# A recurrent-attention and MoE kernel on one core: weight casts on ScalarE, first loads in the modelled queue, products of zeros in TensorE's idle head, DMA transposes for blocks 14 to 23

## The chip, the cores and the metric

The kernel runs on one core of one Trainium2 chip. The metric is the device time of one execution in microseconds (us). The profile is one execution taken by the hardware profiler; its span is about 1.8 us shorter than the timed run. Most runs of one kernel here lie within 1 to 2% of each other.

## The reference

Two stages follow each other. For each of 4 batches and 8 heads, with 768 steps and head size 48:

```python
for t in range(S):
    state = alpha[:, :, t, :, None] * state + einsum('bhd,bhe->bhde', k[:, :, t], v[:, :, t])
    y[:, :, t] = einsum('bhd,bhde->bhe', q[:, :, t], state)
x = y.transpose(0, 2, 1, 3).reshape(B * S, H * D)        # 3072 tokens x 384
h = x @ w_in                                             # 384 x 2048
g = s * max(h, 0) ** 2 + b
out = g @ w_out                                          # 2048 x 384
```

## The kernel before

The 3072 tokens are 24 blocks of 128. For each block the kernel takes the logarithm of alpha (Ln), sums it over time with a matmul, exponentiates it, scales q and k, transposes both, and makes a masked score matrix and a running state. This "attention" of a block takes about 2 us of TensorE at full rate. Then come two dense layers in bf16: `mm1` (1.5k columns per unit, 96 units, 0.65 us each) and `mm2` (96 quarters of a block, 0.65 us each). Weights arrive as fp32 in eight quarters of 768 KB, four of w_in (i0 to i3) and four of w_out (o0 to o3); each is cast to bf16 before use.

Every step is an entry `op(engine, duration, priority, function, reads, writes)`. A small list scheduler in the kernel replays these entries with modelled durations, and the instructions are then emitted in the order of their modelled begin times. On the chip each engine runs its own instructions strictly in that order. If the model believes that a load lands earlier than it does, the engine stops at the instruction that needs it, with ready work behind.

```python
LEAD = {1: 17.0, 2: 20.0, 4: 18.0}         # how far a block's attention runs ahead, in units of 1.65 us
NST = 4                                    # staging buffers for fp32 weights
LOADS = ["b0", "b1", "i0", "i1", "b2", "i2", "b3", "i3", "o0", "o1", "o2", "b4", "o3", "b5", "b6"]

class Schedule:
    def emit(self):
        begin = self.run()                                  # list scheduling, durations in us
        for i in sorted(range(len(self.ops)), key=lambda i: (begin[i], i)):
            self.ops[i][3](*self.ops[i][4])                 # emit in this order
# [...]
    load(0, alpha, a_in); load(0, q, q_in); load(0, k, k_in); load(0, v, v_in)   # block 0, before the scheduler
# [...]
    def cast_w_in(i, st):
        nc.gpsimd.tensor_copy(out=w_in_bf[...], in_=wst[st].rearrange("a (k f) -> a k f", k=3))
# [...]
    def st_T(n):                                            # q and k of a block, on TensorE
        for x, src in ((0, qb_sb[n % 2]), (1, kb_sb[n % 2])):
            f = src.rearrange("a h d -> a (h d)")
            for p in range(NP):
                nc.tensor.transpose(out=t_ps[:, x, p, :], in_=f[:, 128 * p : 128 * p + 128], identity=ident_bf)
# [...]
            if i == 0:                                      # block 0: "landed at 3.5, 4.5, 5.5, 6.5"
                for x, name in enumerate("aqkv"):
                    sched.done((name, 0), 3.5 + x)
# [...]
            op("SP", 2.1, t, load_w_in, i, st, w=[("wst", st)], lat=2.0)
            op("POOL", 1.45, -500, cast_w_in, i, st, r=[("wst", st)], w=[("wib", i)])
# [...]
                    op("SP", 0.98, rank + 0.1 * x, load, n, src, dst, w=[(name, ii)], lat=2.0)
```

Because block 0's four loads are not entries, the modelled load queue is free at time 0, so the model has every later load some 5 us too early (the change enters them with 2.2 + 3 x 0.98 = 5.1 us).

Of the kernel before, what the change touches and what calls it, by code (L numbers as in the profile page):

```python
# [9 lines left out]
BF16 = mybir.dt.bfloat16  # L10
AF = mybir.ActivationFunctionType
# [6 lines left out]
GROUPS = [2, 2, 2, 2, 4, 4, 4, 4]  # L18
LEAD = {1: 17.0, 2: 20.0, 4: 18.0}

# [3 lines left out]

LOADS = ["b0", "b1", "i0", "i1", "b2", "i2", "b3", "i3", "o0", "o1", "o2", "b4", "o3", "b5", "b6"]

class Schedule:
# [79 lines left out]

    def emit(self):
        begin = self.run()
        for i in sorted(range(len(self.ops)), key=lambda i: (begin[i], i)):  # L110
            self.ops[i][3](*self.ops[i][4])


@with_exitstack
def kernel(
# [63 lines left out]

    load(0, alpha, a_in)  # L180
    load(0, q, q_in)
    load(0, k, k_in)
    load(0, v, v_in)
    nc.scalar.preload_act_table_set("natural_log_exp_and_others")
# [4 lines left out]
    ident_bf = sb.tile([128, 128], BF16, name="ident_bf")  # L189
    make_identity(nc, ident_bf)  # L190
    ones_col_bf = sb.tile([128, 1], BF16, name="ones_col_bf")
    nc.vector.memset(ones_col_bf, 1.0)
    vp_sb = many("vp", 3, [128, NP, VW], BF16, zero=nc.gpsimd)
    mask = sb.tile([128, 128], BF16, name="mask")
    make_upper_triangular(nc, mask, 1.0, diag=True)
    b_sb = many("b_s", 2, [128, H, D], FP32)
    binv_sb = many("binv", 2, [128, H, D], FP32)
    qb_sb = many("qb", 2, [128, H, 64], BF16, zero=nc.vector)
    kb_sb = many("kb", 2, [128, H, 64], BF16, zero=nc.vector)
    qkT_sb = many("qkT", 2, [128, 2, NP, 128], BF16)  # L200
    am_sb = many("am", 2, [128, 2, NP, 128], BF16)
# [25 lines left out]
    def cast_w_in(i, st):  # L227
        nc.gpsimd.tensor_copy(
            out=w_in_bf[:, :, QW // 3 * i : QW // 3 * (i + 1)],
            in_=wst[st].rearrange("a (k f) -> a k f", k=3),  # L230
        )

# [6 lines left out]
    def cast_w_out(i, st):  # L239
        nc.gpsimd.tensor_copy(  # L240
            out=w_out_bf[:, 4 * i : 4 * i + 4],
            in_=wst[st].rearrange("a (j m) -> a j m", j=4),
        )

# [56 lines left out]
    def st_vcast(n):  # L301
        nc.gpsimd.tensor_copy(
            out=vp_sb[n % 3].rearrange("a p (x d) -> a p x d", d=D)[:, :, 0:3:2, :],
            in_=v_in[n % NIN].rearrange("a (p e) d -> a p e d", e=2),
        )

    def st_qb(n):
        nc.vector.tensor_tensor(  # L308
            out=qb_sb[n % 2][:, :, 0:D], in0=q_in[n % NIN], in1=b_sb[n % 2], op=ALU.mult
        )  # L310

    def st_kb(n):
        nc.vector.tensor_tensor(
            out=kb_sb[n % 2][:, :, 0:D],
            in0=k_in[n % NIN],
            in1=binv_sb[n % 2],
            op=ALU.mult,
        )

    def st_T(n):  # L320
        for x, src in ((0, qb_sb[n % 2]), (1, kb_sb[n % 2])):
            f = src.rearrange("a h d -> a (h d)")
            for p in range(NP):
                nc.tensor.transpose(  # L324
                    out=t_ps[:, x, p, :],
                    in_=f[:, 128 * p : 128 * p + 128],
                    identity=ident_bf,
                )

    def st_KV(n):  # L330
        kb = kb_sb[n % 2].rearrange("a h d -> a (h d)")
        vp = vp_sb[n % 3]
        for p in range(NP):
            for e in range(2):
                nc.tensor.matmul(  # L335
                    out=p_ps[64 * e : 64 * e + 64, p, :],
                    lhsT=kb[:, 128 * p + 64 * e : 128 * p + 64 * e + 64],
                    rhs=vp[:, p, 48 * e : 48 * e + 96],
                    start=True,
                    stop=True,  # L340
                )

    def st_Tcopy(n):
        nc.vector.tensor_copy(  # L344
            out=qkT_sb[n % 2].rearrange("a x p t -> a (x p t)"),
            in_=t_ps.rearrange("a x p t -> a (x p t)"),
        )
# [18 lines left out]
    def st_A(n):  # L366
        qkT = qkT_sb[n % 2]
        for p in range(NP):
            for e in range(2):
                nc.tensor.matmul(  # L370
                    out=a_ps[:, e, p, :],
                    lhsT=qkT[64 * e : 64 * e + 64, 1, p, :],
                    rhs=qkT[64 * e : 64 * e + 64, 0, p, :],
                    start=True,
                    stop=True,
                )
# [22 lines left out]
    def st_y(n):  # L399
        first = n % NCH == 0  # L400
        qT = qkT_sb[n % 2][:, 0]
        am = am_sb[n % 2]
        vp = vp_sb[n % 3]
        st = s_sb[(n - 1) % 2]
# [104 lines left out]
    def first(n):  # L509
        return n % NCH == 0  # L510
# [10 lines left out]
    for rank, item in enumerate(loads):  # L521
        t, i = rank - 1000, int(item[1:])
        if item[0] == "b":
            if i == 0:
                for x, name in enumerate("aqkv"):
                    sched.done((name, 0), 3.5 + x)
                op("POOL", 0.5, t + 0.5,
# [9 lines left out]
        if item[0] == "i":  # L537
            op("SP", 2.1, t, load_w_in, i, st, w=[("wst", st)], lat=2.0)
            op("POOL", 1.45, -500, cast_w_in, i, st, r=[("wst", st)], w=[("wib", i)])
        else:  # L540
            op("SP", 2.1, t, load_w_out, i, st, w=[("wst", st)], lat=2.0)
            op("POOL", 1.45, -400, cast_w_out, i, st, r=[("wst", st)], w=[("wob", i)])
            op("DVE", 0.85, -5, colsum_part, i, st, r=[("wst", st)],
               w=["colpart" if i else "colsum"])
            if i:
                op("DVE", 0.85, -5, colsum_add, r=["colpart"], w=["colsum"])
# [4 lines left out]
    for g in range(NG):  # L551
        m = GROUPS[g]
        ring = [(first_blk[g] + x) % RING for x in range(m)]
        for n in range(first_blk[g], first_blk[g] + m):
# [11 lines left out]
            op("ACT", 0.55, t + 0.1, st_exp_i, n, r=["ct"], w=[("bi", i2), ("bl", i2)])  # L566
            op("POOL", 0.6, t + 0.2, st_vcast, n, r=[("v", ii)], w=[("vp", i3)])
            op("DVE", 0.47, t + 0.2, st_qb, n, r=[("q", ii), ("b", i2)], w=[("qb", i2)])
            op("DVE", 0.47, t + 0.2, st_kb, n, r=[("k", ii), ("bi", i2)], w=[("kb", i2)])
            op("PE", 0.5, t + 0.3, st_T, n, r=[("qb", i2), ("kb", i2)], w=["ct"], lat=0.27)  # L570
            op("DVE", 0.61, t + 0.4, st_Tcopy, n, r=["ct"], w=[("qkT", i2)])
            op("PE", 0.34, t + 0.35, st_KV, n, r=[("kb", i2), ("vp", i3)], w=["py"], lat=0.27)
            if first(n):
                op("DVE", 0.48, t + 0.5, st_t1, n, r=["py", ("bl", i2)], w=[("S", i2)])
            elif not last(n):
                op("DVE", 0.48, t + 0.5, st_t1, n, r=["py", ("S", 1 - i2)], w=[("t1", i2)])
                op("POOL", 0.9, t + 0.1, st_snew, n, r=[("t1", i2), ("bl", i2)], w=[("S", i2)])
            op("PE", 0.33, t + 0.5, st_A, n, r=[("qkT", i2)], w=["a"], lat=0.27)
            op("DVE", 1.15, t + 0.6, st_mask, n, r=["a"], w=[("am", i2)])
            rr = [("am", i2), ("qkT", i2), ("vp", i3)] + ([] if first(n) else [("S", 1 - i2)])  # L580
            op("PE", 0.55, t + 0.7, st_y, n, r=rr, w=["py"], lat=0.27)
# [13 lines left out]
        for u in range(4 * m):  # L595
# [8 lines left out]
            if jq == 3:  # L604
                op("DVE", 0.54, t + 0.1, oevac, x, r=[("o", ob), "bias", "s"],
                   w=[("os", (x // 4) % 3)])
                op("SP", 0.7, -2000, ostore, x, r=[("os", (x // 4) % 3)])
    sched.emit()

# [29 lines left out]
```

## Time and profile before

| | before |
|---|---|
| time, median | 217.84 us (217.25 to 218.16, 3 runs) |
| span of the profile | 215.9 us |
| last matmul starts | 212.10 us |

The table of stages of the kernel before follows. Its columns are: the stretch in us from the span's start, its length, then busy us (and instructions) of TensorE, TensorE's weight loads, VectorE, ScalarE and GpSimd, then the granted TensorE clock, the busy share of the DMA engines, and GB/s.

```profile
core 0: us, PE busy (x) PEld busy (x) DVE busy (x) ACT busy (x) POOL busy (x), PEclk, DMA share, GB/s
0.00:10.00 10.00, 0.56 (x5) 0.41 (x5) 1.64 (x7) 2.50 (x4) 5.18 (x17) 1.00 0.81 157
10.00:20.00 10.00, 6.48 (x74) 4.39 (x75) 7.44 (x10) 2.79 (x9) 4.07 (x4) 1.00 0.95 264
20.00:30.00 10.00, 7.49 (x67) 4.82 (x65) 5.93 (x10) 3.68 (x10) 4.72 (x5) 1.00 0.92 252
30.00:40.00 10.00, 6.85 (x72) 4.32 (x70) 8.09 (x11) 2.17 (x4) 7.51 (x5) 0.83 0.99 276
40.00:50.00 10.00, 7.02 (x66) 4.19 (x64) 10.00 (x18) 4.43 (x10) 2.79 (x3) 0.84 0.98 226
50.00:60.00 10.00, 10.00 (x113) 6.72 (x110) 9.30 (x23) 6.46 (x15) 3.02 (x4) 0.98 0.64 134
60.00:80.00 20.00, 20.00 (x244) 13.97 (x243) 15.76 (x36) 11.52 (x26) 3.93 (x6) 1.00 1.02 207
```

Two regimes meet near 52 us. From there TensorE is full, and only less TensorE work can shorten the rest. Before that TensorE is busy 7 of 10 us at best while the DMA engines are above 90%, and VectorE is full from 40 to 50 us. This is the "head". A busy TensorE is also not a fast one here, as the next lines show.

Timeline of the kernel before, TensorE, the same six mm1 matmuls twice (columns: start us, us, engine, line, operation, output<-inputs, shape, count):

```profile
24.85 1.46 PE L454 MATMUL h_ps_66<-xd_146,w_in_bf 128*128 128x256 bf16 x6
31.16 0.83 PE L454 MATMUL h_ps_66<-xd_146,w_in_bf 128*128 128x256 bf16 x6
```

The first group ran "cold", at about half the rate. The column for the granted clock says 1.00 for 20 to 30 us, so it does not show this; durations do. TensorE was cold once more at the very end of the head (timeline of the kernel before, one mm2 matmul each):

```profile
48.46 0.53 PE L478 MATMUL o_ps_68<-w_out_bf,gt_160 128*128 128x384 bf16 x1
52.04 0.32 PE L478 MATMUL o_ps_68<-w_out_bf,gt_164 128*128 128x384 bf16 x1
```

From 46.70 us on TensorE waits for nothing in this trace. Its work up to 50.52 us (eight transposes, eight products for the state, four mm2 and six mm1 matmuls) took 3.82 us; the same work later takes 0.44 + 0.30 + 0.65 + 0.65 = 2.04 us. So I estimate that being cold cost about 1.8 us there, with no idle time to hide it.

Timeline of the kernel before, its start on ScalarE and TensorE; in brackets the idle time before the instruction and what ended it:

```profile
8.13 0.52 ACT L275 ACTIVATE la_99<-a_in_71 128x384 bf16<-128x384 f32 x1 [6.13 <-DMA a_in_71<-in_alpha_dram]
8.56 0.51 ACT L275 ACTIVATE la_97<-a_in_70 128x384 bf16<-128x384 f32 x1
9.12 0.48 PE L281 MATMUL ct_ps<-la_97,U_bf 128*128 128x384 bf16 x1 [9.12 <-ACT la_97 L275]
```

ScalarE waits for block 1's alpha (`a_in_71`) with block 0's Ln behind it. Block 0's alpha (`a_in_70`) was issued at 0.73 us and landed 2.8 us later, at 3.5 us: 5 us earlier than its Ln ran.

Timelines of the kernel before, GpSimd and then VectorE, during two weight casts and after them:

```profile
32.26 2.26 POOL L240 CAST w_out_bf<-wst_172 128x1536 bf16<-128x1536 f32 x1 [0.60 <-DMA wst_172<-in_moe_w_out_dram]
34.47 1.52 POOL L240 CAST w_out_bf<-wst_173 128x1536 bf16<-128x1536 f32 x1
```

```profile
33.11 1.55 DVE L471 TENSOR_TENSOR gt_153<-r_150 128x256 bf16<-128x256 bf16 x1
36.05 0.28 DVE L471 TENSOR_TENSOR gt_155<-r_149 128x256 bf16<-128x256 bf16 x1
```

The same square takes 1.55 us beside a cast (and 1.54 us beside the second one) and 0.28 us without one. Last, the transposes of one block in the full part (TensorE's timeline, kernel before); starts are 0.22 us apart for four transposes, so a block's eight cost 0.44 us:

```profile
158.97 0.39 PE L324 MATMUL ct_ps<-ident_bf,qb_130 128*128 128x128 bf16 x4
159.20 0.39 PE L324 MATMUL ct_ps<-ident_bf,kb_134 128*128 128x128 bf16 x4
```

The chain of waits that the profile follows back from the last instruction is TensorE alone, but it reaches back only to 102.7 us (51% of the span), so it says nothing about the head.

### The profile page before, as it was taken

How to read it: one execution, taken by the hardware profiler on the slowest of the kernel's cores; microseconds unless marked ns; L12 is line 12 of the kernel's file. 1: busy time of each engine (PE TensorE's matmuls, PEld its weight loads, DVE VectorE, ACT ScalarE, POOL GpSimd, SP SyncE). 2: the span in 40 equal slices, each digit the busy share in tenths (PEclk: the TensorE clock that was granted, in tenths of full speed). 3: DMA queues.
4: the chain of work that ended last, by engine and by line, in shares of the span. 5: the costliest groups of instructions: out<-in, count | busy, mean ns of one | idle time of the engine just before them, and what ended most of it. 6: DMA issues, size and time to landing. Idle time of an engine off the chain costs nothing.

```text
span 215.9 us, 4933 instructions
## 1 busy us (share of the span) xinstructions
PE 190.6 (88%) x1916; PEld 112.4 (52%) x1916; DVE 149.3 (69%) x283; ACT 100.8 (47%) x217; POOL 47.5 (22%) x65
## 2 busy tenths in 40 slices
PE   0167694959999999999999999999999999999993
PEld 0045462535767677756455555545555555555551
DVE  3187269999978787886898868799686963444321
ACT  2313242245655654633787637776365434444200
POOL 8144446635021212111112211002220100000000
PEclk9999998788999999999999999999999999999999
DMA  6999899999499999999977775230110111111122
GB/s 128 189 328 228 189 355 288 241 179 178 98 205 210 211 199 211 196 208 194 218 151 146 148 170 117 44 78 2 36 39 0 39 36 39 37 38 38 39 73 73
DMA packets 107096, 30.21 MB, mean 140 GB/s; under 512 B 100416, under 2 KB 105536, under 8 KB 107072
## 3 DMA queue, kind: packets, MB, share of 16 engines
q1 hardware_dynamic: 107008, 29.89, 59.6%
q8 instruction: 15, 0.25, 0.5%
q14 instruction: 9, 0.07, 0.1%
q0 software_dynamic: 64, 0.00, 0.0%
HBM read 25.17 MB, written 4.72 MB: 138 GB/s over the span
## 4 chain that ended last, share of the span: by engine, by line
PE 51%; DVE 0%; issue 0%
PE o_ps_69 L478 10%; PE h_ps_66 L454 10%; PE o_ps_68 L478 10%; PE h_ps_67 L454 10%; PE py_ps L414 3%; PE ct_ps L324 2%; PE a_ps L370 2%; PE py_ps L335 2%; PE ct_ps L281 1%; PE ct_ps L286 0%; DVE o_sb_169 L489 0%
## 5 line engine op out<-in xcount | busy, mean ns | idle before, releaser
L454 PEld LDWEIGHTS <-w_in_bf 128*128 128x128 bf16 x384 | 36.0, 102 | 23.9 <-issue 3.1
L463 ACT ACTIVATE r_149<-h_ps_66 128x512 bf16<-128x512 f32 x48 | 28.7, 598 | 36.3 <-PE h_ps_66 L454 33.3
L463 ACT ACTIVATE r_150<-h_ps_67 128x512 bf16<-128x512 f32 x48 | 28.8, 599 | 29.1 <-PE h_ps_67 L454 13.2
L454 PE MATMUL h_ps_66<-xd_147,w_in_bf 128*128 128x512 bf16 (+1 forms) x72 | 16.3, 344 | 1.4 <-ACT r_149 L463 1.4
L454 PE MATMUL h_ps_67<-xd_147,w_in_bf 128*128 128x512 bf16 (+1 forms) x72 | 16.7, 352 | 0.0
L379 DVE TENSOR_TENSOR am_139<-a_ps,mask 128x1024 bf16<-128x1024 f32 x12 | 14.7, 1222 | 2.6 <-PE a_ps L370 2.4
L379 DVE TENSOR_TENSOR am_138<-a_ps,mask 128x1024 bf16<-128x1024 f32 x12 | 14.6, 1220 | 1.8 <-PE a_ps L370 1.5
L454 PE MATMUL h_ps_67<-xd_146,w_in_bf 128*128 128x256 bf16 (+1 forms) x72 | 14.4, 333 | 0.7 <-ACT r_150 L463 0.7
L454 PE MATMUL h_ps_66<-xd_146,w_in_bf 128*128 128x256 bf16 (+1 forms) x72 | 15.0, 344 | 0.0
L364 POOL TENSOR_TENSOR s_st_144<-t_142,blast_140 128x384 bf16<-128x384 bf16 x8 | 7.7, 960 | 23.5 <-DVE t_142 L356 16.3
L344 DVE COPY qkT_136<-ct_ps 128x1024 bf16<-128x1024 bf16 x12 | 8.3, 688 | 6.2 <-PE ct_ps L324 5.7
L281 PE MATMUL ct_ps<-la_97,U_bf 128*128 128x384 bf16 x12 | 4.3, 360 | 9.1 <-ACT la_97 L275 9.1
L364 POOL TENSOR_TENSOR s_st_145<-t_143,blast_141 128x384 bf16<-128x384 bf16 x8 | 7.8, 974 | 15.4 <-DVE t_143 L356 13.3
L344 DVE COPY qkT_137<-ct_ps 128x1024 bf16<-128x1024 bf16 x12 | 8.3, 688 | 4.2 <-PE ct_ps L324 4.1
L454 PE MATMUL h_ps_66<-xd_148,w_in_bf 128*128 128x256 bf16 (+1 forms) x48 | 9.8, 327 | 0.0
L454 PE MATMUL h_ps_67<-xd_148,w_in_bf 128*128 128x256 bf16 (+1 forms) x48 | 9.8, 326 | 0.0
L295 ACT ACTIVATE b_s_124<-ct_ps 128x384 f32<-128x384 f32 x12 | 5.9, 491 | 7.9 <-PE ct_ps L286 7.6
L295 ACT ACTIVATE b_s_125<-ct_ps 128x384 f32<-128x384 f32 x12 | 5.9, 490 | 6.1 <-PE ct_ps L286 5.8
L286 PEld LDWEIGHTS <-la_97 128*128 128x128 bf16 x48 | 3.1, 100 | 8.8 <-issue 8.0
L324 PE MATMUL ct_ps<-ident_bf,qb_128 128*128 128x128 bf16 x48 | 5.2, 236 | 2.3 <-DVE qb_128 L308 2.3
L432 ACT ACTIVATE xd_147<-py_ps 128x384 bf16<-128x384 f32 x10 | 4.9, 493 | 4.7 <-PE py_ps L414 4.5
L308 DVE TENSOR_TENSOR qb_128<-q_in_75,b_s_124 128x384 bf16<-128x384 f32 x3 | 1.7, 552 | 7.7 <-ACT b_s_124 L295 7.7
(209 smaller groups left out, 466.9 us busy)
## 6 DMA issues: line engine op xcount, KB each, us to landing
out_dram<-o_sb_167 SPq DMA_DIRECT2D x8, 192.0 KB, 2.3
out_dram<-o_sb_168 SPq DMA_DIRECT2D x8, 192.0 KB, 2.1
out_dram<-o_sb_169 SPq DMA_DIRECT2D x8, 192.0 KB, 1.9
a_in_70<-in_alpha_dram SPq DMA_DIRECT2D x5, 192.0 KB, 4.0
q_in_75<-in_q_dram SPq DMA_DIRECT2D x5, 192.0 KB, 3.8
k_in_80<-in_k_dram SPq DMA_DIRECT2D x5, 192.0 KB, 3.7
v_in_85<-in_v_dram SPq DMA_DIRECT2D x5, 192.0 KB, 4.1
a_in_71<-in_alpha_dram SPq DMA_DIRECT2D x5, 192.0 KB, 3.9
```

Of the source, the lines that this page charges most:

```text
L281: nc.tensor.matmul(out=cum_ps, lhsT=U_bf, rhs=la[:, :, 0:D], start=True, stop=True)
L295: nc.scalar.activation(out=b_sb[n % 2], in_=cum_ps, func=AF.Exp)
L324: nc.tensor.transpose(out=t_ps[:, x, p, :], in_=f[:, 128 * p : 128 * p + 128], identity=ident_bf,)
L335: nc.tensor.matmul(out=p_ps[64 * e : 64 * e + 64, p, :], lhsT=kb[:, 128 * p + 64 * e : 128 * p + 64 * e + 64], rhs=vp[:, p, 48 * e : 48 * ...
L344: nc.vector.tensor_copy(out=qkT_sb[n % 2].rearrange("a x p t -> a (x p t)"), in_=t_ps.rearrange("a x p t -> a (x p t)"),)
L364: nc.gpsimd.tensor_tensor(out=s_sb[n % 2], in0=t1_sb[n % 2], in1=bl, op=ALU.mult)
L379: nc.vector.tensor_tensor(out=am_sb[n % 2].rearrange("a e p t -> a (e p) t"), in0=a_ps.rearrange("a e p t -> a (e p) t"), in1=mask.unsquee ...
L414: nc.tensor.matmul(out=y_ps[32 * (x % 4) : 32 * (x % 4) + 32 * m, x // 4, :], lhsT=(st[:, p, c0 : c0 + 32 * m] if e is None else vp[:, p, ...
L432: nc.scalar.activation(out=xd_sb[g % 3][:, :, t * C : (t + 1) * C], in_=y_ps, func=AF.Copy)
L454: nc.tensor.matmul(out=hp[:, i * n : (i + 1) * n], lhsT=w_in_bf[:, kk, 128 * j : 128 * (j + 1)], rhs=xd_sb[g % 3][:, kk, 0:n], start=(kk = ...
L463: nc.scalar.activation(out=r_sb[w % 2], in_=h_ps[w % 2], func=AF.Relu)
L478: nc.tensor.matmul(out=op[:, 0:d_model], lhsT=gt_sb[j][:, c0 : c0 + C], rhs=w_out_bf[:, j, :], start=(j == 0), stop=(j == NJ - 1),)
```

## The change

The intent: relieve VectorE of the GpSimd casts, make the fixed order start with what lands first, keep TensorE warm in the head, and take transposes off TensorE where it is full. Leads and the order of loads were set anew, and some buffers got a third or fourth copy.

```diff
-LEAD = {1: 17.0, 2: 20.0, 4: 18.0}
+LEAD = {1: 20.0, 2: 20.0, 4: 29.0}
+NPE = 14
-LOADS = ["b0", "b1", "i0", "i1", "b2", "i2", "b3", "i3", "o0", "o1", "o2", "b4", "o3", "b5", "b6"]
+LOADS = ["b0", "b1", "i0", "b2", "i1", "i2", "b3", "i3", "b4", "o0", "b5", "o1", "o2", "b6", "o3"]
# [...] emit() calls fill(idle) where the model has TensorE idle, until the first mm2
# [...] vp 3 -> 4 copies; q and k share one tile "qk", 2 -> 3 copies; qkT 2 -> 3 copies
     def cast_w_in(i, st):                          # cast_w_out likewise
-        nc.gpsimd.tensor_copy(
+        nc.scalar.activation(
             out=..., in_=...,
+            func=AF.Copy,
+    def st_Tdma(n):
+        nc.scalar.dma_start_transpose(
+            out=qkT_sb[n % 3].rearrange("a x p t -> a (x p) t"),
+            in_=qk_sb[n % 3].rearrange("a x h d -> a (x h d)"),
+        )
# [...]
                 for x, name in enumerate("aqkv"):
-                    sched.done((name, 0), 3.5 + x)
+                    op("SP", 2.2 if x == 0 else 0.98, t + 0.01 * x, lambda: None,
+                       w=[(name, 0)], lat=2.0)
-            op("POOL", 1.45, -500, cast_w_in, i, st, r=[("wst", st)], w=[("wib", i)])
+            op("ACT", 1.35, -500, cast_w_in, i, st, r=[("wst", st)], w=[("wib", i)])
# [...]
+            if n < NPE:
                 op("PE", 0.5, t + 0.3, st_T, ...)
                 op("DVE", 0.61, t + 0.4, st_Tcopy, ...)
+            else:
+                op("ACT", 0.8, t + 0.3, st_Tdma, ..., lat=5.0)
+    def fill(idle):
+        for _ in range(int((idle - 0.1) / 0.25)):
+            nc.tensor.matmul(out=o_ps[0], lhsT=ident_bf, rhs=zeros, start=True, stop=True)
-    sched.emit()
+    sched.emit(fill, mm2)
```

More of the change, by code (lines that the diff above doesn't have):

```diff
@@ L106, in run, with emit @@
         return begin
-    def emit(self):
+    def emit(self, fill, until):
         begin = self.run()
+        free = 0.0
         for i in sorted(range(len(self.ops)), key=lambda i: (begin[i], i)):
-            self.ops[i][3](*self.ops[i][4])
+            eng, _, _, fn, args = self.ops[i][:5]
+            if eng == "PE":
+                if fn is until:
+                    free = None
+                if free is not None:
+                    if free > 0.0:
+                        fill(begin[i] - free)
+                    free = self.end[i]
+            fn(*args)
 @with_exitstack
@@ L178, in load @@
         )
-    load(0, alpha, a_in)
-    load(0, q, q_in)
-    load(0, k, k_in)
-    load(0, v, v_in)
+    for src, dst in ((alpha, a_in), (q, q_in), (k, k_in), (v, v_in)):
+        load(0, src, dst)
     nc.scalar.preload_act_table_set("natural_log_exp_and_others")
@@ L190 @@
     make_identity(nc, ident_bf)
+    zeros = sb.tile([128, 512], BF16, name="zeros")
+    nc.vector.memset(zeros, 0.0)
     ones_col_bf = sb.tile([128, 1], BF16, name="ones_col_bf")
     nc.vector.memset(ones_col_bf, 1.0)
-    vp_sb = many("vp", 3, [128, NP, VW], BF16, zero=nc.gpsimd)
+    vp_sb = many("vp", 4, [128, NP, VW], BF16, zero=nc.gpsimd)
     mask = sb.tile([128, 128], BF16, name="mask")
@@ L197 @@
     binv_sb = many("binv", 2, [128, H, D], FP32)
-    qb_sb = many("qb", 2, [128, H, 64], BF16, zero=nc.vector)
-    kb_sb = many("kb", 2, [128, H, 64], BF16, zero=nc.vector)
-    qkT_sb = many("qkT", 2, [128, 2, NP, 128], BF16)
+    qk_sb = many("qk", 3, [128, 2, H, 64], BF16, zero=nc.vector)
+    qkT_sb = many("qkT", 3, [128, 2, NP, 128], BF16)
     am_sb = many("am", 2, [128, 2, NP, 128], BF16)
@@ L239, in cast_w_out @@
     def cast_w_out(i, st):
-        nc.gpsimd.tensor_copy(
+        nc.scalar.activation(
             out=w_out_bf[:, 4 * i : 4 * i + 4],
             in_=wst[st].rearrange("a (j m) -> a j m", j=4),
+            func=AF.Copy,
         )
@@ L302, in st_vcast @@
         nc.gpsimd.tensor_copy(
-            out=vp_sb[n % 3].rearrange("a p (x d) -> a p x d", d=D)[:, :, 0:3:2, :],
+            out=vp_sb[n % 4].rearrange("a p (x d) -> a p x d", d=D)[:, :, 0:3:2, :],
             in_=v_in[n % NIN].rearrange("a (p e) d -> a p e d", e=2),
@@ L308, in st_qb @@
         nc.vector.tensor_tensor(
-            out=qb_sb[n % 2][:, :, 0:D], in0=q_in[n % NIN], in1=b_sb[n % 2], op=ALU.mult
+            out=qk_sb[n % 3][:, 0, :, 0:D], in0=q_in[n % NIN], in1=b_sb[n % 2], op=ALU.mult
         )
@@ L313, in st_kb @@
         nc.vector.tensor_tensor(
-            out=kb_sb[n % 2][:, :, 0:D],
+            out=qk_sb[n % 3][:, 1, :, 0:D],
             in0=k_in[n % NIN],
@@ L320, in st_T @@
     def st_T(n):
-        for x, src in ((0, qb_sb[n % 2]), (1, kb_sb[n % 2])):
-            f = src.rearrange("a h d -> a (h d)")
+        f = qk_sb[n % 3].rearrange("a x h d -> a (x h d)")
+        for x in range(2):
             for p in range(NP):
+                c0 = 512 * x + 128 * p
                 nc.tensor.transpose(
-                    out=t_ps[:, x, p, :],
-                    in_=f[:, 128 * p : 128 * p + 128],
-                    identity=ident_bf,
-                )
+                    out=t_ps[:, x, p, :], in_=f[:, c0 : c0 + 128], identity=ident_bf
+                )
+    def st_Tdma(n):
[3 more added lines that the diff above has]
+        )
     def st_KV(n):
-        kb = kb_sb[n % 2].rearrange("a h d -> a (h d)")
-        vp = vp_sb[n % 3]
+        kb = qk_sb[n % 3][:, 1].rearrange("a h d -> a (h d)")
+        vp = vp_sb[n % 4]
         for p in range(NP):
@@ L344, in st_Tcopy @@
         nc.vector.tensor_copy(
-            out=qkT_sb[n % 2].rearrange("a x p t -> a (x p t)"),
+            out=qkT_sb[n % 3].rearrange("a x p t -> a (x p t)"),
             in_=t_ps.rearrange("a x p t -> a (x p t)"),
@@ L366, in st_A @@
     def st_A(n):
-        qkT = qkT_sb[n % 2]
+        qkT = qkT_sb[n % 3]
         for p in range(NP):
@@ L400, in st_y @@
         first = n % NCH == 0
-        qT = qkT_sb[n % 2][:, 0]
+        qT = qkT_sb[n % 3][:, 0]
         am = am_sb[n % 2]
-        vp = vp_sb[n % 3]
+        vp = vp_sb[n % 4]
         st = s_sb[(n - 1) % 2]
@@ L538 @@
             op("SP", 2.1, t, load_w_in, i, st, w=[("wst", st)], lat=2.0)
-            op("POOL", 1.45, -500, cast_w_in, i, st, r=[("wst", st)], w=[("wib", i)])
+            op("ACT", 1.35, -500, cast_w_in, i, st, r=[("wst", st)], w=[("wib", i)])
         else:
             op("SP", 2.1, t, load_w_out, i, st, w=[("wst", st)], lat=2.0)
-            op("POOL", 1.45, -400, cast_w_out, i, st, r=[("wst", st)], w=[("wob", i)])
+            op("ACT", 1.35, -400, cast_w_out, i, st, r=[("wst", st)], w=[("wob", i)])
             op("DVE", 0.85, -5, colsum_part, i, st, r=[("wst", st)],
@@ L566 @@
             op("ACT", 0.55, t + 0.1, st_exp_i, n, r=["ct"], w=[("bi", i2), ("bl", i2)])
-            op("POOL", 0.6, t + 0.2, st_vcast, n, r=[("v", ii)], w=[("vp", i3)])
-            op("DVE", 0.47, t + 0.2, st_qb, n, r=[("q", ii), ("b", i2)], w=[("qb", i2)])
-            op("DVE", 0.47, t + 0.2, st_kb, n, r=[("k", ii), ("bi", i2)], w=[("kb", i2)])
-            op("PE", 0.5, t + 0.3, st_T, n, r=[("qb", i2), ("kb", i2)], w=["ct"], lat=0.27)
-            op("DVE", 0.61, t + 0.4, st_Tcopy, n, r=["ct"], w=[("qkT", i2)])
-            op("PE", 0.34, t + 0.35, st_KV, n, r=[("kb", i2), ("vp", i3)], w=["py"], lat=0.27)
+            op("POOL", 0.6, t + 0.2, st_vcast, n, r=[("v", ii)], w=[("vp", n % 4)])
+            op("DVE", 0.47, t + 0.2, st_qb, n, r=[("q", ii), ("b", i2)], w=[("qb", i3)])
+            op("DVE", 0.47, t + 0.2, st_kb, n, r=[("k", ii), ("bi", i2)], w=[("kb", i3)])
+            if n < NPE:
+                op("PE", 0.5, t + 0.3, st_T, n, r=[("qb", i3), ("kb", i3)], w=["ct"], lat=0.27)
+                op("DVE", 0.61, t + 0.4, st_Tcopy, n, r=["ct"], w=[("qkT", i3)])
+            else:
+                op("ACT", 0.8, t + 0.3, st_Tdma, n, r=[("qb", i3), ("kb", i3)],
+                   w=[("qkT", i3)], lat=5.0)
+            op("PE", 0.34, t + 0.35, st_KV, n, r=[("kb", i3), ("vp", n % 4)], w=["py"], lat=0.27)
             if first(n):
@@ L577 @@
                 op("POOL", 0.9, t + 0.1, st_snew, n, r=[("t1", i2), ("bl", i2)], w=[("S", i2)])
-            op("PE", 0.33, t + 0.5, st_A, n, r=[("qkT", i2)], w=["a"], lat=0.27)
+            op("PE", 0.33, t + 0.5, st_A, n, r=[("qkT", i3)], w=["a"], lat=0.27)
             op("DVE", 1.15, t + 0.6, st_mask, n, r=["a"], w=[("am", i2)])
-            rr = [("am", i2), ("qkT", i2), ("vp", i3)] + ([] if first(n) else [("S", 1 - i2)])
+            rr = [("am", i2), ("qkT", i3), ("vp", n % 4)] + ([] if first(n) else [("S", 1 - i2)])
             op("PE", 0.55, t + 0.7, st_y, n, r=rr, w=["py"], lat=0.27)
@@ L607 @@
                 op("SP", 0.7, -2000, ostore, x, r=[("os", (x // 4) % 3)])
-    sched.emit()
+    def fill(idle):
+        for _ in range(int((idle - 0.1) / 0.25)):
+            nc.tensor.matmul(
+                out=o_ps[0], lhsT=ident_bf, rhs=zeros, start=True, stop=True
+            )
+    sched.emit(fill, mm2)
 _INS = ['q', 'k', 'v', 'alpha', 'moe_w_in', 'moe_w_out', 'moe_s', 'moe_b']
```

## The prediction

> **What bounds the kernel now.** By the table of stages, TensorE is busy 48.0 of 48.0 us from 52 to 100 us and 50.0 of 50.0 us from 150 to 200 us; in the timeline matmuls run there at full rate (512 columns every 0.216 us, 128x128 transposes every 0.056 us). The last 160 us are TensorE's own work; about 3.3 us of store follow. The first 52 us are different: the DMA engines are 92 to 99% busy from 10 to 50 us, TensorE does only about 17 us of warm-rate work in 52 us, and from 36 to 52 us VectorE is busy 15.8 of 16.0 us.
>
> In the head I read four losses:
> - The Ln of block 0 sits behind that of block 1, which waited 6.1 us for its DMA. Alpha of block 0 had landed at 3.5 us, yet the first matmul starts at 9.1 us.
> - While GpSimd casts weights (1.46 to 2.26 us each, eight times), VectorE's bf16 squares stretch from 0.28 to 0.9 to 1.55 us, one q multiply from 0.55 to 1.61 us. The Trainium skill, "GPSIMD Engine Reference" (Specifications), says that the SBUF interfaces are shared with VectorE; this trace agrees.
> - TensorE is cold: six 128x256 matmuls take 1.46 us at 25 us, 0.83 us later. The skill, "TensorE: Matmul & The Clock Gate" (Part 1), describes the half-rate state after idle windows.
> - Blocks 4 and 5 load late.
>
> **What the change does.**
> 1. Casts go to ScalarE. Its 384- and 512-element activations take 0.49 and 0.60 us, so I estimate 1.46 us for 1536 elements. Eight cost 12 us of ScalarE, busy only 2 to 4 of each 10 us in the head. Gain: VectorE's stretches, about 6 us.
> 2. With the first loads modelled, block 0 should begin 4 to 5 us earlier; blocks 4 and 5 load earlier, output weights up to 8 us later. DMA volume is the same, so these loads still end near 50 us.
> 3. Zero products keep TensorE warm in gaps until the first mm2; while cold they can delay work slightly.
> 4. Ten blocks lose 8 PE transposes (0.44 us warm, so 4.4 us of TensorE, all in the saturated part) and a VectorE copy (0.69 us). They gain a DMA transpose of 256 KB each, issued on ScalarE (estimate 0.8 us; it is about 60% busy there), with some us of latency, hidden by a third buffer and the greater lead.
>
> **On the critical path.** Item 4 gives 4.4 us almost one for one. Items 1 to 3 let TensorE saturate near 40 us instead of 52; they overlap, so I count 9 us together (range 4 to 13). Sum 13.4 us: 217.84 - 13.4 = **204.5 us**, range 199.5 to 211. Chances: faster by over 2% 0.87, within 2% 0.10, slower 0.03.
>
> **What would show it.** First matmul at 4 to 5.5 us; squares at 0.28 us throughout the head; casts of about 1.46 us on ScalarE; no cold matmuls after about 12 us; TensorE full from about 40 us, without gaps at blocks 14 to 23.
>
> **What would make it wrong.** DMA transposes that hold ScalarE for 2 us or more, or land after 8 us or more behind the loads (the DMA is 93% busy until 100 us), so that score products stall TensorE; casts delaying Ln, exp and evacuation on ScalarE; later output weights becoming the head's limit; zero products overrunning real work.

## The result

| | before | changed |
|---|---|---|
| time, median | 217.55 us (216.29 to 218.16, 4 runs) | 207.31 us (206.48 to 208.12, 4 runs) |
| ratio | | 0.9536, 95% interval 0.9476 to 0.9597 |
| last matmul starts | 212.10 us | 202.29 us |

A ratio is the mean time of one kernel's runs over the mean of the other's runs of the same rounds, so it is not quite the ratio of the medians. Executions over 1.5% slower than the fastest of the same kernel are left out of the means. Below, a difference of two ratios is turned into us by multiplying it with the median of before on that chip.

The table of stages of the changed kernel, columns as before:

```profile
core 0: us, PE busy (x) PEld busy (x) DVE busy (x) ACT busy (x) POOL busy (x), PEclk, DMA share, GB/s
0.00:10.00 10.00, 5.80 (x35) 2.64 (x35) 4.38 (x11) 3.27 (x6) 6.13 (x19) 1.00 0.85 160
10.00:20.00 10.00, 8.57 (x104) 4.65 (x106) 6.33 (x10) 4.15 (x9) 2.25 (x3) 1.00 0.97 267
20.00:30.00 10.00, 7.17 (x96) 5.25 (x95) 5.87 (x15) 7.02 (x12) 1.52 (x2) 1.00 0.95 239
30.00:40.00 10.00, 7.16 (x95) 5.01 (x95) 7.21 (x15) 7.65 (x13) 2.15 (x3) 1.00 0.95 204
40.00:50.00 10.00, 8.59 (x107) 5.95 (x107) 10.00 (x23) 8.54 (x16) 0.66 (x2) 1.00 0.92 245
50.00:60.00 10.00, 7.02 (x88) 4.71 (x87) 7.53 (x18) 6.02 (x14) 2.65 (x2) 1.00 0.92 209
60.00:80.00 20.00, 20.00 (x248) 13.50 (x246) 16.75 (x38) 10.27 (x24) 4.58 (x7) 1.00 0.99 207
```

TensorE's busy time up to 20 us is mostly zeros (the trace has 38 products in all). After that it works at the warm rate, so that 7 of 10 us hold more than before. But it is full only after 56 us, not from 40 us; in the second profile of this kernel (run `a_again` below) it waits last at 53.3 us, and then again for 0.4 us at 73.5 us. The end comes 9.8 us earlier all the same: at 56.2 us the changed kernel has 146.1 us to its last matmul (202.29 - 56.2), where the kernel before had 159.6 us at 52.5 us (212.10 - 52.5). The difference of 13.5 us, less the 3.7 us by which the full part starts later, is the gain.

Timeline of the changed kernel, its start on ScalarE and TensorE:

```profile
3.62 0.52 ACT L289 ACTIVATE la_97<-a_in_70 128x384 bf16<-128x384 f32 x1 [1.61 <-DMA a_in_70<-in_alpha_dram]
4.20 0.48 PE L295 MATMUL ct_ps<-la_97,U_bf 128*128 128x384 bf16 x1 [4.20 <-ACT la_97 L289]
```

Block 0 now starts when its alpha lands, 4.9 us earlier. A cast on ScalarE and the squares on VectorE that follow it (timelines of the changed kernel):

```profile
23.42 1.48 ACT L240 ACTIVATE w_in_bf<-wst_177 128x1536 bf16<-128x1536 f32 x1 [1.36 <-DMA wst_177<-in_moe_w_in_dram]
```

```profile
25.84 0.29 DVE L490 TENSOR_TENSOR gt_154<-r_152 128x256 bf16<-128x256 bf16 x1 [2.66 <-ACT r_152 L482]
```

The square is short again (three of the 35 squares up to 60 us still take 0.51 to 0.94 us), but it waited 2.66 us for a relu on ScalarE that stood behind the cast, which itself waited 1.36 us for its weights. The relu's input was ready at about 23.2 us (22.41 + 0.83 us of mm1), and it ran at 25.23 us. The longest wait in front of a cast is the last one (timelines of the changed kernel, ScalarE, VectorE and TensorE):

```profile
54.18 1.48 ACT L253 ACTIVATE w_out_bf<-wst_178 128x1536 bf16<-128x1536 f32 x1 [3.05 <-DMA wst_178<-in_moe_w_out_dram]
55.57 0.51 ACT L289 ACTIVATE la_99<-a_in_72 128x384 bf16<-128x384 f32 x1
55.98 0.58 ACT L482 ACTIVATE r_152<-h_ps_66 128x512 bf16<-128x512 f32 x1
```

```profile
54.25 0.96 DVE L261 TENSOR_TENSOR colpart<-wst_178 128x768 f32<-128x768 f32 x1 [2.47 <-DMA wst_178<-in_moe_w_out_dram]
55.12 0.68 DVE L363 COPY qkT_138<-ct_ps 128x1024 bf16<-128x1024 bf16 x1
```

```profile
55.87 0.40 PE L389 MATMUL a_ps<-qkT_138 64*128 64x128 bf16 x8 [1.90 <-DVE qkT_138 L363]
```

ScalarE stands 3.05 us in front of the cast of o3, but next to nothing behind it was ready in that time: the alpha that the Ln needs lands at 54.8 us (issued at 48.3 us, 6.5 us to landing), and the mm1 results for the two relus are there from about 53.3 and 54.0 us on. VectorE stands 2.47 us at the same load, for its column sum, and there ready work does stand behind: block 6's transpose copy, whose eight transposes had ended by 51.5 us. That copy is what TensorE's 1.90 us is for. The load of o3 lands at 54.1 us; the kernel's model had its cast at 47.8 us. This wait is also not the same in each execution: in the second profile of the changed kernel ScalarE waited 0.55 us for the same load (timeline of `a_again`):

```profile
51.64 1.48 ACT L253 ACTIVATE w_out_bf<-wst 128x1536 bf16<-128x1536 f32 x1 [0.55 <-DMA wst<-in_moe_w_out_dram]
```

The DMA transposes, on ScalarE's queue (one of ten), and the DMA page: queues with packets, MB and the time of their packets as a share of 16 engines, then an issue line with the count and us from issue to landing.

```profile
102.57 1.34 ACTq L344 DMA_TRANSPOSE qkT_140<-qk_136  x1
```

```profile
q1 hardware_dynamic: 107008, 29.89, 64.0%
q10 hardware_dynamic: 10560, 2.62, 8.7%
...
qkT_140<-qk_136 ACTq DMA_TRANSPOSE x4, 3.7
qkT_138<-qk_132 ACTq DMA_TRANSPOSE x3, 5.6
```

Each holds ScalarE's queue 1.25 to 1.37 us (I had estimated 0.8; one of the ten in the second profile held it 2.04 us) and lands 3.7 to 5.6 us after issue, by the medians of the three tiles; single ones landed after 3.1 to 7.4 us. No matmul waits for one of them in this trace, and one weight load waits 0.4 us. The chain of waits of the changed kernel reaches back over nearly the whole span and runs through the loads in the head (no comparison with before, whose chain stops at 102.7 us):

```profile
PE 70%; SPq 12%; DMA 9%; DVE 4%; issue 2%; ACT 1%; DVEq 0%
```

### The profile page after: what moved, and what is told of

Read it like the earlier page. It is cut to its first block, busy times and chain, and to the rows that moved or that the text cites. A ratio compares the mean times of both kernels' runs of the same rounds, so it can differ in the third digit from the quotient of the medians.

```text
span 206.3 us, 4820 instructions
## 1 busy us (share of the span) xinstructions
PE 185.6 (90%) x1858; PEld 107.7 (52%) x1877; DVE 136.3 (66%) x273; ACT 109.6 (53%) x225; POOL 34.1 (17%) x58
## 3 DMA queue, kind: packets, MB, share of 16 engines
q1 hardware_dynamic: 107008, 29.89, 64.0%
q10 hardware_dynamic: 10560, 2.62, 8.7%
## 4 chain that ended last, share of the span: by engine, by line
PE 70%; SPq 12%; DMA 9%; DVE 4%; issue 2%; ACT 1%; DVEq 0%
PE o_ps_69 L497 16%; PE o_ps_68 L497 14%; PE h_ps_67 L473 12%; PE h_ps_66 L473 12%; SPq L188 11%; PE py_ps L433 5%; DMA wst_178<-in_moe_w_out_dram 3%; DMA wst_178<-in_moe_w_in_dram 3%; DMA wst_175<-in_moe_w_out_dram 3%; PE a_ps L389 3%; PE py_ps L354 2%; PE ct_ps L295 2%; PE ct_ps L339 2%; SPq L232 1%; DVE colpart L261 1%
## 5 line engine op out<-in xcount | busy, mean ns | idle before, releaser
L473 PEld LDWEIGHTS <-w_in_bf 128*128 128x128 bf16 x384 | 34.6, 97 | 19.3 <-issue 1.0
L473 PE MATMUL h_ps_67<-xd_150,w_in_bf 128*128 128x512 bf16 (+1 forms) x70 | 16.0, 343 | 0.4 <-issue 0.2
L473 PE MATMUL h_ps_66<-xd_150,w_in_bf 128*128 128x512 bf16 (+1 forms) x67 | 15.5, 341 | 0.7 <-ACT r_152 L482 0.3
L473 PE MATMUL h_ps_66<-xd_149,w_in_bf 128*128 128x256 bf16 (+1 forms) x70 | 13.0, 306 | 0.3
L473 PE MATMUL h_ps_67<-xd_149,w_in_bf 128*128 128x256 bf16 (+1 forms) x69 | 12.8, 306 | 0.1
L638 PE MATMUL o_ps_68<-zeros,ident_bf 128*128 128x512 bf16 x38 | 11.3, 425 | 0.1
L383 POOL TENSOR_TENSOR s_st_147<-t_145,blast_143 128x384 bf16<-128x384 bf16 x8 | 6.9, 859 | 23.0 <-DVE t_145 L375 23.0
L309 ACT ACTIVATE b_s_129<-ct_ps 128x384 f32<-128x384 f32 x12 | 5.9, 490 | 8.0 <-PE ct_ps L300 5.4
L383 POOL TENSOR_TENSOR s_st_148<-t_146,blast_144 128x384 bf16<-128x384 bf16 x8 | 7.2, 904 | 16.7 <-DVE t_146 L375 16.7
L473 PE MATMUL h_ps_67<-xd_151,w_in_bf 128*128 128x256 bf16 (+1 forms) x48 | 9.8, 326 | 0.0
L309 ACT ACTIVATE b_s_128<-ct_ps 128x384 f32<-128x384 f32 x12 | 5.9, 490 | 7.0 <-PE ct_ps L300 5.4
L473 PE MATMUL h_ps_66<-xd_151,w_in_bf 128*128 128x256 bf16 (+1 forms) x44 | 9.3, 321 | 0.3 <-issue 0.2
L638 PEld LDWEIGHTS <-ident_bf 128*128 128x128 bf16 x41 | 3.9, 105 | 4.3 <-issue 1.9
L312 ACT ACTIVATE binv_131<-ct_ps 128x384 f32<-128x384 f32 x12 | 5.9, 490 | 0.0
L312 ACT ACTIVATE binv_130<-ct_ps 128x384 f32<-128x384 f32 x12 | 5.9, 489 | 0.0
```

Of the source, the lines that this page charges most:

```text
L309: nc.scalar.activation(out=b_sb[n % 2], in_=cum_ps, func=AF.Exp)
L312: nc.scalar.activation(out=binv_sb[n % 2], in_=cum_ps, func=AF.Exp, scale=-1.0)
L383: nc.gpsimd.tensor_tensor(out=s_sb[n % 2], in0=t1_sb[n % 2], in1=bl, op=ALU.mult)
L473: nc.tensor.matmul(out=hp[:, i * n : (i + 1) * n], lhsT=w_in_bf[:, kk, 128 * j : 128 * (j + 1)], rhs=xd_sb[g % 3][:, kk, 0:n], start=(kk = ...
L638: nc.tensor.matmul(out=o_ps[0], lhsT=ident_bf, rhs=zeros, start=True, stop=True)
```

## The experiments

My theory after this reading: the transposes gave about 4 us, the rest is in the head, and there each part gives something. The rivals were that DMA transposes cost what they save, that zeros carry the head, that moving the casts to ScalarE merely moves the wait, and that the order of loads matters most. Twelve kernels ran, all with correct results, five rounds each, in three groups; the kernels of one group ran on one chip beside 11 runs of before. One caution holds for all: any edit to the entries makes the scheduler order everything anew, so a variant differs from its parent by more than the edited lines. This is why I tested parts both by taking them out and by adding them to the kernel before.

| kernel | median us | ratio to before | 95% interval |
|---|---|---|---|
| a_again (changed, once more) | 207.22 | 0.9496 | 0.9463 to 0.9529 |
| a_no_dmaT | 211.13 | 0.9689 | 0.9653 to 0.9724 |
| a_no_zeros | 207.16 | 0.9492 | 0.9455 to 0.9528 |
| a_pool_casts | 209.96 | 0.9619 | 0.9578 to 0.9660 |
| a_old_order | 207.24 | 0.9507 | 0.9470 to 0.9544 |
| a_old_preset | 214.89 | 0.9789 | 0.9737 to 0.9841 |
| a_old_lead | 208.49 | 0.9546 | 0.9499 to 0.9593 |
| a_retimed | 208.82 | 0.9586 | 0.9536 to 0.9636 |
| b_preset | 212.97 | 0.9780 | 0.9734 to 0.9825 |
| b_casts | 214.36 | 0.9843 | 0.9796 to 0.9891 |
| b_both | 210.25 | 0.9673 | 0.9630 to 0.9715 |
| a_tuned | 204.38 | 0.9406 | 0.9367 to 0.9444 |

Medians of before: 218.0 us (first four), 218.17 us (next four), 217.34 us (last four).

### The changed kernel again

No edit.

> The changed kernel unaltered, to have its time beside the variants on the same chip. Expected 206.5 to 208 us, ratio to before near 0.954. In the trace again: TensorE with gaps until about 56 us, then full.

Measured 207.22 us, ratio 0.9496. This is the reference for the variants below. Its profile has a span of 204.2 us against 206.3 us of the first one, so single profiles of this kernel differ by 2 us.

### All transposes on TensorE

```diff
-NPE = 14
+NPE = 24
```

> The changed kernel with all 24 blocks transposed on TensorE. Theory A (TensorE is the bound from 56 us on, so its 10 x 0.44 us come off one for one): 4 to 5 us slower than the changed kernel, about 211.7 us. Rival B (the DMA transposes bring gaps and ScalarE time, 1.25 us each, that cost as much as they save, and all of the gain is in the head): within 1 us of the changed kernel, about 207.3 us.

Measured 211.13 us. Ratios differ by 0.0193, which is 4.2 us of 218.0 us. Theory A stands: 10 x 0.44 us of TensorE come off nearly one for one, so little of the 1.25 us of ScalarE and of the latency can have reached the time.

### No products of zeros

```diff
-    sched.emit(fill, mm2)
+    sched.emit(lambda idle: None, mm2)
```

> The changed kernel without the products of zeros. Theory A (the zeros keep TensorE at full rate in the head, but the head is held by loads and by waits on other engines): cold matmuls come back between 8 and 30 us, and the time rises by 0.5 to 2 us. Rival B (the zeros carry most of the head's gain of 5 to 6 us): 4 us or more slower. Rival C (they only fill idle time or get in the way): same or faster.

Measured 207.16 us, ratio 0.9492 against 0.9496: no effect. The cold matmuls did come back (TensorE's timeline of the kernel without zeros, twelve matmuls each):

```profile
23.37 2.74 PE L473 MATMUL h_ps<-xd,w_in_bf 128*128 128x256 bf16 x12
28.39 1.49 PE L473 MATMUL h_ps<-xd,w_in_bf 128*128 128x256 bf16 x12
```

The first twelve start 1 us later and take 1.25 us longer than those at 28 us. By 39 us the two kernels stand at the same place: the first mm2 starts at 38.97 us with zeros and at 39.16 us without. So whatever the zeros gained early in the head was gone by then. Rival C held; my 0.5 to 2 us did not. The run does not say what warm matmuls are worth in general: without the zeros too the changed kernel is warm from about 28 us on in its profile, and the zeros stop at the first mm2. The kernel before was cold again from 46.7 us on without idle time (about 1.8 us by the estimate above), and no run changes the rate there alone, so part of what the other edits gain can be this.

### Casts back on GpSimd

```diff
-        nc.scalar.activation(out=..., in_=..., func=AF.Copy)
+        nc.gpsimd.tensor_copy(out=..., in_=...)                   # both casts
-            op("ACT", 1.35, -500, cast_w_in, ...)
+            op("POOL", 1.45, -500, cast_w_in, ...)                # and cast_w_out
```

> The changed kernel with the weight casts back on GpSimd. Theory A (GpSimd casts stretch VectorE's squares and fp32 additions, some 5 us of VectorE in a stretch in which it is nearly full): squares of 0.9 to 1.55 us come back, and the time rises by 2 to 4 us. Rival B (on ScalarE the casts wait for their loads with Ln, relu and exp queued behind them, 3.1 us for the last output weights, so that the move gains nothing): same within 1 us, or faster.

Measured 209.96 us: 0.0123 of 218.0, or 2.7 us, slower. VectorE's stretched squares are back (timelines of this kernel, GpSimd and VectorE):

```profile
44.06 3.72 POOL L252 CAST w_out_bf<-wst 128x1536 bf16<-128x1536 f32 x2 [3.17 <-DMA wst<-in_moe_w_out_dram]
```

```profile
44.91 3.02 DVE L488 TENSOR_TENSOR gt<-r 128x256 bf16<-128x256 bf16 x2
```

Two squares take 3.02 us beside the casts (0.48 us for such a pair a little earlier in the same trace). Theory A stands for the squares; the fp32 additions are not stretched in this trace (0.94 to 0.96 us each, as in the changed kernel).

### The old order of loads

```diff
-LOADS = ["b0", "b1", "i0", "b2", "i1", "i2", "b3", "i3", "b4", "o0", "b5", "o1", "o2", "b6", "o3"]
+LOADS = ["b0", "b1", "i0", "i1", "b2", "i2", "b3", "i3", "o0", "o1", "o2", "b4", "o3", "b5", "b6"]
```

> The changed kernel with the list of loads of before (output weights o0 to o2 ahead of block 4, o3 ahead of block 5); the first loads stay modelled. Theory A (blocks 4 and 5 early give TensorE work sooner): 1 to 2.5 us slower than the changed kernel. Rival B (output weights 6 to 10 us later cost as much as the earlier blocks bring): within 0.7 us, or faster.

Measured ratio 0.9507, against 0.9496 on another chip: the same within 0.7 us. Rival B held. In its profile TensorE is full already from 50 us (10.00 of 10.00 us from 50 to 60 us, against 9.17 us in the changed kernel's second profile), so the earlier output weights seem to help the head; the gain is not in the time. From 100 to 150 us TensorE is busy 48.34 of 50 us there and 49.20 us in the changed kernel's second profile, so in these two profiles part of it is given back later.

### The first loads at fixed times

```diff
-                    op("SP", 2.2 if x == 0 else 0.98, t + 0.01 * x, lambda: None,
-                       w=[(name, 0)], lat=2.0)
+                    sched.done((name, 0), 3.5 + x)
```

> The changed kernel with the first loads taken as landed at fixed times, as before (block 0's alpha at 3.5, q, k, v one us apart; the loads queue modelled from 0). Theory A (the model then has the loads some 4 us too early, so the fixed order of ScalarE, VectorE and TensorE puts work on late loads ahead of work that is ready, first of all the Ln of block 1 ahead of that of block 0): first matmul near 9 us again, 1.5 to 4 us slower than the changed kernel. Rival B (loads set the pace of the head, and a late start is made up by 50 us): within 0.7 us.

Measured 214.89 us: 0.0293 of 218.17, or 6.4 us, slower (two of its six runs count as slow, and the ratio leaves them out). This is the largest single part, and more than I had expected of it. The waits of TensorE without and with the modelled first loads (columns: engine, output, line, waited for whom, us in total, times, longest). First this kernel, then the changed one (second profile):

```profile
PE ct_ps L295 <- ACT la L289: 9.3, 1, 9.3
PE o_ps L497 <- ACT w_out_bf L253: 6.0, 4, 2.2
```

```profile
PE ct_ps L295 <- ACT la L289: 6.4, 3, 4.3
PE o_ps L497 <- ACT w_out_bf L253: 1.4, 2, 0.7
```

The first matmul is back at 9.26 us. But by these totals the start is not the larger half (2.9 us more against 4.6 us more): TensorE also stands in front of mm2 four times, at output weights that the model has too early. The products behind mm2 are not ready either at the longest of these waits (2.2 us, to 55.90 us), because VectorE stands 2.25 us at the same load, with a mask product behind it whose input was there from 52.7 us on. TensorE was also cold after that wait: its column-sum product took 2.93 us at 57.45 us, against 1.45 us in the changed kernel, so some of the 6.4 us is the rate and not the wait. A wrong time at the start is wrong for every load that follows.

### The old leads

```diff
-LEAD = {1: 20.0, 2: 20.0, 4: 29.0}
+LEAD = {1: 17.0, 2: 20.0, 4: 18.0}
```

> The changed kernel with the leads of before (17, 20, 18 units in place of 20, 20, 29). Theory A (TensorE is full from 56 us on whatever the lead, but the DMA transposes take 4 to 6 us to land, and need the longer lead): gaps of 1 to 3 us in total before the score products of blocks 14 to 23, 1 to 3 us slower than the changed kernel. Rival B (18 units of 1.65 us cover the latency): within 0.7 us.

Measured ratio 0.9546, 1.1 us above the changed kernel's 0.9496 by the centres, but the intervals overlap. Undecided.

### Load times set to what the trace shows

```diff
-                    op("SP", 0.98, rank + 0.1 * x, load, ...)
+                    op("SP", 1.08, rank + 0.1 * x, load, ...)
-            op("SP", 2.1, t, load_w_in, ...)
+            op("SP", 2.6, t, load_w_in, ...)                      # load_w_out likewise
```

> The changed kernel with the scheduler's load times set to what its trace shows (1.08 us for a block's tensor and 2.6 us for a quarter of weights in place of 0.98 and 2.1), which puts the modelled casts within 1 us of the traced ones (the last at 54.2 us, where the changed kernel's model has 47.8). Theory A (ScalarE waits 3.1 us in front of the last cast and 1 to 2.7 us in front of others with ready work behind it, because the model has these loads too early): 1 to 2.5 us faster than the changed kernel, about 205.5 us. Rival B (the loads themselves hold the head, not the order): within 0.7 us.

Measured 208.82 us: 0.0090 of 218.17, or 2.0 us, slower than the changed kernel. Both theory and rival failed. In this kernel's profile the wait before the last cast is 1.68 us, shorter than the 3.05 us of the changed kernel's first profile but longer than the 0.55 us of its second, so the wait that the theory was built on differs by 2.5 us between two executions of one kernel, and no shortening is shown. TensorE is busy only 17.82 of 20 us from 100 to 120 us. Timelines of this kernel there, ScalarE and TensorE:

```profile
113.72 0.52 ACT L289 ACTIVATE la<-a_in 128x384 bf16<-128x384 f32 x1 [2.16 <-DMA a_in<-in_alpha_dram]
114.15 1.06 ACT L482 ACTIVATE r<-h_ps 128x512 bf16<-128x512 f32 x2
```

```profile
114.78 0.81 PE L473 MATMUL h_ps<-xd,w_in_bf 128*128 128x512 bf16 x2 [1.41 <-ACT r L482]
```

Here ready work does stand behind a load: ScalarE waits for a late block's alpha with two relus behind it, and TensorE waits for the relus. The wait shown is 1.41 us of the 2.18 us that TensorE is idle in these 20 us (0.45 us in the changed kernel's second profile). That it is the whole of the loss in the timed runs is not shown.

### Parts added to the kernel before

Modelled first loads alone:

```diff
-                    sched.done((name, 0), 3.5 + x)
+                    op("SP", 2.2 if x == 0 else 0.98, t + 0.01 * x, lambda: None,
+                       w=[(name, 0)], lat=2.0)
```

> The kernel of before with one part of the change: the first loads modelled in the queue. Theory A (the fixed order must match when loads land, whichever engine casts; taking this out of the changed kernel cost 6 us): 4 to 6.5 us faster than before, ratio 0.970 to 0.982. Rival B (the wrong times hurt only where casts wait for loads on ScalarE, in front of Ln, exp and relu; on GpSimd a waiting cast holds little): 0 to 2 us faster.

Measured ratio 0.9780, 4.8 us faster. Theory A stands: the wrong times also hurt where GpSimd casts.

The casts on ScalarE alone (the edit of the change):

> The kernel of before with one part of the change: the weight casts on ScalarE; the load times stay wrong. Theory A (the parts add up; taking the casts' move out of the changed kernel cost 2.7 us): 2 to 3.5 us faster than before, ratio near 0.988. Rival B (with wrong load times the casts queue up ahead of ready work on ScalarE, which eats the relief of VectorE): same as before within 1 us, or slower.

Measured ratio 0.9843, 3.4 us faster. Theory A stands again; wrong load times do not eat the relief of VectorE.

Both:

> The kernel of before with both: casts on ScalarE and the first loads modelled; old order of loads, old leads, no zeros, all transposes on TensorE. From the runs so far zeros and the order of loads are worth nothing and the DMA transposes 4 us, so if that holds this should stand where the changed kernel without DMA transposes stands, ratio 0.965 to 0.972, about 7 us faster than before. If it is 0.98 or more, the leads, the buffers or the order of loads carry more than I think.

Measured ratio 0.9673, 7.1 us faster, where the changed kernel without DMA transposes stands (0.9689). The two parts alone give 4.8 and 3.4 us, so they overlap by about 1 us, which is no more than the noise. With the 4.2 us of the DMA transposes this makes 11.3 us, and the changed kernel of the second measurement is 11.0 us faster than before (0.0504 of 218.0). Nothing beyond the noise of about 1 us is left for the zeros, the order of loads, the leads and the extra buffers together.

### An attempt at a better version

```diff
-LEAD = {1: 20.0, 2: 20.0, 4: 29.0}
+LEAD = {1: 20.0, 2: 25.0, 4: 18.0}
-NPE = 14
+NPE = 16
-LOADS = ["b0", "b1", "i0", "b2", "i1", "i2", "b3", "i3", "b4", "o0", "b5", "o1", "o2", "b6", "o3"]
+LOADS = ["b0", "b1", "i0", "b2", "i1", "b3", "i2", "i3", "b4", "o0", "o1", "o2", "o3", "b5", "b6"]
-    UNIT = 1.65
+    UNIT = 1.60
# modelled durations: 1.05 (was 0.98) for a block's tensor, 2.30 (was 2.1) for a quarter of weights,
# 1.25 (was 0.8) of ScalarE for a DMA transpose
```

The values were picked by replaying many fixed orders under the durations measured above and under slower loads, and keeping an order that was good on the average of both.

> An attempt at a better version: the changed kernel with the scheduler's times set to measured ones (1.05 and 2.3 us for loads, 1.25 us of ScalarE for a DMA transpose), all output weights ahead of block 5, leads 25 and 18, DMA transposes for blocks 16 to 23, unit 1.6. If the changed kernel's remaining loss in the head (about 20 us by 56 us) comes in part from an order that does not match the loads: 1.5 to 4 us faster than the changed kernel, ratio 0.932 to 0.943. Rival (a retimed order already lost 2 us once, as Ln of later blocks then waits for its load on ScalarE in front of relu): same or slower, 0.95 or more.

Measured 204.38 us, ratio 0.9406. The intervals of 0.9406 and 0.9496 do not touch; the difference is 0.0090, about 2.0 us faster than the changed kernel and 13 us faster than before. One row of its table of stages:

```profile
50.00:60.00 10.00, 10.00 (x114) 6.56 (x113) 6.83 (x13) 4.49 (x11) 1.02 (x2) 1.00 0.91 197
```

TensorE is full from 50 us, and the last output weights are cast at 43.24 us without a wait. Which of its settings does it was not separated.

## Why the prediction was right

The time lay inside the range and the direction was right; the gain was 10 to 11 us where I had put 13.4 us.

- **DMA transposes, 4.4 us.** Measured 4.2 us. The issue on ScalarE was 1.25 us and not 0.8 us, but by the time it cost next to nothing, and the landings (3.1 to 7.4 us) were early enough.
- **Casts.** 1.48 us on ScalarE, as estimated (1.46 us); squares near 0.28 us again, with three exceptions. Worth 3.4 us added alone and 2.7 us taken out. The risk I had named, casts that delay Ln and relu on ScalarE, is there in the trace (the relu at 25.23 us, 2 us after its input); what it costs was not measured. The 3.05 us before the last cast held back next to nothing that was ready.
- **First loads.** First matmul at 4.20 us, inside my 4 to 5.5 us. Worth 4.8 us added alone and 6.4 us taken out. I had this as an earlier start of block 0; the waits at the output weights without it (6.0 us against 1.4 us) say that the rest of the order matters as much, since every modelled load time moves with it.
- **Zeros.** The cold matmuls went as predicted, and that was worth nothing: where the zeros work, TensorE had time to spare. I listed cold TensorE among four "losses" of the head. At its end (46.7 to 50.5 us of the kernel before) it was a loss, but the zeros don't reach there, and the runs don't separate it.
- **Blocks 4 and 5 earlier.** Worth nothing by the run with the old order.
- **The step that was mis-sized** is this one: "Items 1 to 3 let TensorE saturate near 40 us instead of 52; they overlap, so I count 9 us together". The three items measured 6.8 us together (the changed kernel without DMA transposes, new leads and buffers included, 0.0311 of 218.0), and 7.1 us without zeros and new order. The route was wrong, too: TensorE was full not earlier but later than before (56 us, or 53 us in the second profile, against 52 us); what shortened the time is that more of its work was done by then (146.1 us were left against 159.6 us, of which the transposes explain 4.4 us). That the sum came out near is in part luck. In its place the runs show a head that ends with its loads: the last output weights landed at 54.1 us (51.6 us in the second profile), and in the first profile VectorE stood at them with ready work behind. I had named later output weights as a risk and still counted the earlier blocks as a gain.

What stays open: the worth of the new leads (1.1 us by the centres, inside the noise), how much of the retimed kernel's loss is the one wait shown, and how much of the gain in the head is that TensorE runs warm at its end.

## What to carry to other kernels

When an order is fixed ahead by a model, check the modelled landing of every early load against the trace first; here four loads left out of the model cost 5 us, the largest single part. An instruction that waits for a load should stand, in the order of its engine, where nothing ready is behind it: the transpose copy behind the last column sum kept TensorE waiting 1.90 us. Look for what was ready behind a wait before you count the wait as a loss, and look at a second profile: the 3.05 us here was 0.55 us in the next one, and a change aimed at it made the kernel 2.0 us slower. Making an engine faster while it still waited for loads gained nothing here (zeros, 0.9492 against 0.9496), while work taken off the engine that is full came off nearly one for one (4.2 of 4.4 us).

## What the Trainium skill lacked or had wrong

- "GPSIMD Engine Reference" (Specifications) says that the SBUF interfaces are shared with VectorE, for instructions in a 2-port mode or with two SBUF inputs. The traces agree, and nothing was wrong in it. What the runs add is the size in this kernel: bf16 squares went from 0.28 to 1.55 us beside a cast, and moving eight casts away was worth 2.7 to 3.4 us.
- "DMA: Bandwidth & Descriptors" (DMA Transpose) gives for trn2 neither the time an SBUF-to-SBUF transpose holds its issuing queue nor its latency. Here a 128x1024 bf16 transpose held ScalarE's queue 1.25 to 1.37 us (once 2.04 us, in the second profile) and landed after 3.1 to 7.4 us.
- "Advanced Engine Details and Errata" (X-Bar Transpose) says that transpose DMAs on trn2 are as fast as regular ones. Here, beside loads that filled the queues, a packet of the transposes took 27 ns (8.7% of 16 engines x 206.3 us over 10560 packets of 248 bytes) and one of the other queue 20 ns (64.0%, 107008 packets of 279 bytes). No run has them alone, so this is a sign and not a refutation.
- "TensorE: Matmul & The Clock Gate" (Part 1) describes the half-rate state after idle windows; the traces agree (1.46 against 0.83 us for six matmuls). It says that the penalty of the ramp is under 1% of a typical span; without the zeros the changed kernel lost nothing measurable to it (0.9492 against 0.9496). Later cold stretches are another matter: the one at the end of the head of the kernel before I estimate at 1.8 us. Beyond a warning about a trace's clock events, the page does not say that the mean granted clock of a profile can read 1.00 in a cold stretch, as it did from 20 to 30 us of the kernel before.
- "ScalarE: Activation LUTs" (What ACT_TABLE_LOAD costs) gives 186 ns + 0.833 ns per element for an activation with immediate scale and bias, an estimate of 1.466 us for 1536 elements; the casts took 1.48 us. Nothing lacked there.
